# Attention feeding a gated product: four chunks of Strassen-like products run as one stream, with attention and checks dealt out as timed events

## The chip, the cores and the metric

One core of a Trainium2 chip. The metric is the device time of the whole program in microseconds, the median of the runs. TensorE (PE) does matrix products, VectorE (DVE) and ScalarE (ACT) read its results in PSUM, GpSimd (POOL) works in SBUF alone, and SyncE (SP) issues transfers. PSUM has eight banks, and each holds a tile of 128 x 512 fp32 values.

## The reference

Attention over 4 batches, 8 heads, 768 positions and head width 64, where a position sees the first `n_sink` (4) positions and a window of 128 before it; then a gated product on the result, without a nonlinearity:

```python
scores = np.where(is_sink | in_window, scale * (q @ k.T), -1e9)
a = softmax(scores)            # over the last axis, sum + 1e-9
x = (a @ v)                    # heads joined: 3072 tokens x 512
out = ((x @ w_a) * (x @ w_b)) @ w_out     # 512 -> 1536 -> 512
```

Inputs are fp32; the weights come as 64-bit words that the kernel turns into a high and a low fp16 part.

## The kernel before

Tokens are worked off in seven chunks (`CHUNKS`): 512 tokens, 256, 256, then four of 512. While the gated product of chunk c runs on TensorE, the attention for chunk c+1 is made in between, by a generator (`attention`, `pipeline`) that `run` advances in its function `between` after each group of matmuls. A *unit* of attention is one head and one tile of 128 queries: two score matmuls into the only PSUM bank with tag `s` (L600), on VectorE the mask and maximum (L608, L610), the exponential on ScalarE (L612), sum and reciprocal (L614, L615), the scaling (L620), two units later a transpose through TensorE (L644, L645 or L650, L651), and for each pair of heads the product with v (L515, L658) and the sinks' part (`sinks_t`, `sinks_av`: L665 to L679). GpSimd rounds and splits q and k (L450, L456).

Chunks 0 to 2 use the plain product (`moe`: L1031 the two input products, L1040 the output product), each fp32 product as three of fp16 parts. In chunk 0 the weights are loaded and converted besides, on VectorE and ScalarE (L399 to L419). Chunks 3 to 6 use seven products for a 2 x 2 block product (`moe_of_seven`: L924 the products, L934 the output projections). They need sums of weight blocks: `weight_sums` (L375 to L386) makes them in 84 units, one instruction each, 72 on VectorE and 12 on ScalarE; `ahead` calls for 42 in chunk 1 and 42 in chunk 2. They also need sums of the input's blocks, made by `split_sums` (L886 to L900) at the head of each chunk.

A chunk of seven has six steps p; each has the products 5, 1, 2, 6, 3, 7, 4 (12 matmuls of 256 columns each) into two banks, copies between the banks on ScalarE (L981, L985, L993), the two gates `even` and `odd` (L944 to L949), and their high and low fp16 parts (ScalarE L954, GpSimd L955). `out(i)` puts the four output projections (six matmuls of 512 columns each) of the step before between the products; the first step has none, and after the sixth the last four follow one another. `finish` then moves the four output banks out (L1080), stores them, and the sums of their squares follow in the next chunk (`sum_rows`, L1109).

Instructions stand in each engine's queue in an order that a scheduler works out from the program order and from modelled times: an instruction with nothing to wait for can be put ahead of its place. `keep_in_program_order` (`pin`) binds one behind the instruction written just before it on its engine. An engine works its queue off in order.

`check_weight` loads each weight once more in two halves (L437) and takes minimum and maximum on VectorE (L427, L429): 30 of the 36 in the last chunk, one each 9/5 slots of 66, looked at in the following slot; two in each of chunks 3, 4 and 5. The loads of heads (`kr`, `qr`, `vsr`) and of checks share six SBUF buffers (`io`).

Of the kernel before, what the change touches and what calls it, by code (L numbers as in the profile page):

```python
# [20 lines left out]
P = 128  # L21
# [215 lines left out]
SEVEN = 3  # L237
R = P * 2
RING = 4

class Fast:
# [120 lines left out]
    def weight_sums(self):  # L364

        nc = self.nc
        V = nc.vector
        for p in range(NJ // 2):
            self.sums[p] = self.wp.tile([P, 2, 4, 2, R], F16, tag=f"r{p}", name=f"sums{p}")
            for i, kind in enumerate("ab"):  # L370
                b = self.cp.tile([P, 4, R], F32, tag="blocks", name=f"blocks{kind}{p}")
                t = self.cp.tile([P, 4, R], F32, tag="turns", name=f"turns{kind}{p}")
                for d in range(2):
                    wh, wl = self.weight(kind, 2 * p + d)
                    V.tensor_tensor(b[:, 2 * d:2 * d + 2].rearrange("p a f -> p (a f)"), wh, wl, op=ALU.add)  # L375
                    yield
                V.tensor_tensor(t[:, 0:2], b[:, 2:4], b[:, 0::2], op=ALU.subtract)
# [3 lines left out]
                V.tensor_tensor(t[:, 3], b[:, 1], t[:, 2], op=ALU.subtract)  # L381
# [4 lines left out]
                V.tensor_tensor(s[:, :, 1], t, s[:, :, 0], op=ALU.subtract)  # L386
# [35 lines left out]
    def check_weight(self, kind, j):  # L422

        nc, pin = self.nc, self.tc.keep_in_program_order
        for raw, i in self.unchecked:
# [5 lines left out]
        self.unchecked = []  # L431
        if kind is None:
            return
# [85 lines left out]
    def attention(self, b, t0, nt, xf, heads=range(H), bank=None):  # L519
# [4 lines left out]
        return self.pipeline(units, nt, late, *parts, 2, 4, 1, self.tight)  # L524

    def attentions(self, segments, xf):

        gens, o = [], 0
        for b, t0, nt in segments:
            gens.append(self.attention(b, t0, nt, [x[:, o:o + nt * P] for x in xf]))  # L530
            o += nt * P
        for i, gen in enumerate(gens):
            n = self.steps(segments[i], self.tight) - (i > 0)
            for k in range(n):
                if k == n - 5 and i + 1 < len(gens):
                    next(gens[i + 1])
                next(gen)
                yield
            assert next(gen, "end") == "end"

    def steps(self, segment, apart):
        b, t0, nt = segment
        return H * nt + 7 + (10 if apart else 0)
# [282 lines left out]
    def pipeline(self, units, nt, late, do_prep, scores, transposes, av, sinks_t, sinks_av, lag, group, early, apart):  # L826
# [5 lines left out]
        for k in range(nu + lag + 2 + group // 2):  # L832
# [6 lines left out]
            if 0 <= n < nu and units[n][1] == nt - 1:  # L839
                h = units[n][0]  # L840
                av(h)
                if apart and h % 2:
                    yield
                if h % group == group - 1 and late:
                    sinks_t(h // group)
                    if apart:
                        yield
            for c in range(group // 2):
                n -= 1
                if 0 <= n < nu and units[n][1] == nt - 1:  # L850
                    h = units[n][0]
                    if h % group == group - 1 and late:
                        sinks_av(h // group, c)
                        if apart:
                            yield
# [21 lines left out]
    def split_sums(self, xf, tag):  # L877

        nc = self.nc
        V = nc.vector  # L880
        a11, a12, a21, a22 = (xf[:, 2 * k:2 * k + 2, e::2] for e in range(2) for k in range(2))
        xs = {}
# [11 lines left out]
        s2 = self.mo.tile([P, 2, R], F32, tag="g", name=f"s2_{tag}")  # L894
# [6 lines left out]
        split(7, a21)  # L901
        split(4, a22)
        return xs

    def moe_of_seven(self, segments, first, xf, between, ahead, last):
# [3 lines left out]
        tag = f"{first}"  # L909
        xs = self.split_sums(xf, tag)  # L910
        outs = [self.ps.tile([P, DM], F32, tag=("o0", "o1", "o2", "av")[i], name=f"o{tag}_{i}") for i in range(4)]
        places = []
# [46 lines left out]
        for p in range(NJ // 2):  # L959
# [7 lines left out]
            def out(i):  # L967
                if prev is not None:
                    project(i, *prev)
# [333 lines left out]
```

## Time and profile before

| | us |
|---|---|
| median of 3 runs | 753.59 (752.77 to 754.82) |
| the profiled execution | 755.17 |
| its span | 753.4 |
| TensorE busy | 701.5 |
| VectorE busy | 540.7 |
| ScalarE busy | 418.0 |
| GpSimd busy | 263.0 |

The profile is of one execution. The span runs from the program's first to its last instruction; the execution's own time has 1.8 us around it. Busy times are unions of an engine's instructions. TensorE's instructions overlap, so how fast it works is read from the time from one start to the next, or from runs of matmuls without a gap. Chunk c ends where the first product of the next begins: at 149.9, 231.2, 301.9, 418.6, 537.8 and 651.4 us for chunks 0 to 5, and the last matmul of chunk 6 ends at 746.4.

### The profile page before, as it was taken

Reading aid. Unit: us, or ns where it says so; the run is one execution under the profiler, and the core shown is the slowest. Engines: PE = TensorE matmul, PEld = TensorE weight load, DVE = VectorE, ACT = ScalarE, POOL = GpSimd, SP = SyncE. Lnnn points to the kernel's source line nnn. Section 1 sums busy time; section 2 is a strip of 40 time slices with the busy share of each in tenths; the row PEclk is TensorE's granted clock in tenths of the full one; section 3 lists DMA queues with packets and bytes.
Section 4 is the critical chain, followed back from the end, with each engine's and each line's share of the span. In section 5 each row is a group of like instructions: output and inputs, shape, how many; then the busy total and the mean of one; then the engine's idle time right before and its main releaser. Section 6 shows DMA issues by size and latency. Waiting matters only on the chain. (4 is left out here: it accounts for less than half of the span.)

```text
span 753.4 us, 14486 instructions
## 1 busy us (share of the span) xinstructions
PE 701.5 (93%) x4976; PEld 475.0 (63%) x4976; DVE 540.7 (72%) x1660; ACT 418.0 (55%) x1169; POOL 263.0 (35%) x312
## 2 busy tenths in 40 slices
PE   8999998979889999898999899999899999798996
PEld 5644444456656767676776576767577777576673
DVE  7999999999998565855555765664755653886653
ACT  6867877556447675755644654563666453422222
POOL 2200004127743664354441564673154511111111
PEclk9999999999999999999999999999999999999999
DMA  8566454012311222122110222142112010466521
GB/s 271 192 228 215 156 206 161 18 68 61 92 40 58 71 81 77 44 57 76 37 50 8 96 79 60 37 142 75 57 57 86 22 51 1 140 207 215 184 67 58
DMA packets 43533, 73.43 MB, mean 97 GB/s; under 512 B 4608, under 2 KB 21056, under 8 KB 43456
## 3 DMA queue, kind: packets, MB, share of 16 engines
q1 hardware_dynamic: 40208, 66.96, 28.2%
q10 hardware_dynamic: 3248, 5.51, 1.9%
q8 instruction: 40, 0.66, 0.4%
q14 instruction: 37, 0.30, 0.1%
HBM read 66.16 MB, written 6.29 MB: 96 GB/s over the span
## 5 line engine op out<-in xcount | busy, mean ns | idle before, releaser
L924 PEld LDWEIGHTS <-sums 128*128 128x128 f16 x1152 | 112.4, 99 | 24.2 <-issue 6.7
L934 PE MATMUL o<-wt,gh 128*128 128x512 f16 x384 | 115.2, 379 | 2.9 <-ACT gh L954 2.9
L955 POOL TENSOR_TENSOR gl<-g,gh 128x512 f16<-128x512 f32 x48 | 55.6, 1158 | 168.5 <-ACT gh L954 149.6
L1031 PEld LDWEIGHTS <-wt 128*128 128x128 f16 x864 | 82.9, 99 | 47.6 <-issue 5.7
L924 PEld LDWEIGHTS <-wt 128*128 128x128 f16 x864 | 83.1, 98 | 24.0 <-issue 7.2
L612 ACT ACTIVATE p<-p,st 128x136 f32<-128x136 f32 (+2 forms) x160 | 66.1, 413 | 45.8 <-DVE st L610 41.0
L1031 PE MATMUL b<-x,wt 128*128 128x256 f16 (+1 forms) x432 | 73.3, 312 | 3.5 <-DVE st L614 3.2
L924 PE MATMUL x<-x,sums 128*128 128x256 f16 x576 | 73.3, 275 | 3.6 <-DVE g L948 3.6
L924 PE MATMUL x<-x,wt 128*128 128x256 f16 x576 | 72.6, 273 | 2.6 <-ACT z L985 2.6
L934 PE MATMUL o<-wt,gl 128*128 128x512 f16 x192 | 72.8, 379 | 2.0 <-POOL gl L955 2.0
L1031 PE MATMUL a<-x,wt 128*128 128x256 f16 (+1 forms) x432 | 72.7, 309 | 1.9 <-ACT wt L414 1.4
L450 POOL TENSOR_SCALAR qh<-qr 128x256 fp32r<-128x256 f32 (+1 forms) x48 | 26.2, 545 | 135.9 <-PE s L600 94.1
L924 PE MATMUL z<-x,sums 128*128 128x256 f16 x576 | 73.4, 274 | 0.0
L600 PE MATMUL s<-ks,qh 128*128 128x264 f32 (+1 forms) x160 | 61.5, 384 | 9.4 <-DVE st L610 8.3
L620 ACT ACTIVATE p<-p,st 128x128 f32<-128x128 f32 x120 | 47.9, 399 | 35.5 <-DVE st L615 34.8
L954 ACT CAST gh<-g 128x512 f16<-128x512 f32 x48 | 29.6, 616 | 64.2 <-DVE g L949 55.5
L1040 PE MATMUL o<-wt,gh 128*128 128x512 f16 x192 | 60.3, 387 | 2.4 <-ACT wt L414 1.0
L456 POOL TENSOR_TENSOR ks<-kr,ks 64x400 fp32r<-64x400 f32 (+1 forms) x48 | 61.0, 1271 | 3.7
L608 DVE COPY_PREDICATED s<-mg,s 128x128 f32<-128x128 int32 x120 | 34.6, 288 | 32.7 <-PE s L600 32.7
L645 DVE TENSOR_TENSOR pt<-t,tri 128x256 f32<-128x256 f32 x120 | 50.1, 417 | 9.4 <-PE t L644 8.8
L934 PEld LDWEIGHTS <-gh 128*128 128x128 f16 x384 | 37.1, 99 | 31.0 <-ACT gh L954 4.3
L614 DVE TENSOR_SCALAR st<-st 128x1 f32<-128x1 f32 x160 | 23.9, 150 | 36.6 <-ACT p L612 36.0
(187 smaller groups left out, 1450.4 us busy)
## 6 DMA issues: line engine op xcount, KB each, us to landing
raw<-in_wa_dram SPq DMA_DIRECT2D x12, 512.0 KB, 4.6
raw<-in_wb_dram SPq DMA_DIRECT2D x12, 512.0 KB, 4.6
raw<-in_wo_dram SPq DMA_DIRECT2D x12, 512.0 KB, 4.3
qr<-in_qT_dram SPq DMA_DIRECT2D x24, 256.0 KB, 2.6
chk_b<-in_wb_dram SPq DMA_DIRECT2D x24, 256.0 KB, 3.2
chk_o<-in_wo_dram SPq DMA_DIRECT2D x24, 256.0 KB, 3.5
chk_a<-in_wa_dram SPq DMA_DIRECT2D x24, 256.0 KB, 3.3
out_dram<-os ACTq DMA_DIRECT2D x20, 256.0 KB, 2.1
```

What stands on the lines that cost most here:

```text
L456: self.nc.gpsimd.tensor_tensor(o, i, high.bitcast(F32), op=ALU.subtract)
L600: mm = nc.tensor.matmul(ps[:, :w], lhsT=q[:, i * P:(i + 1) * P], rhs=ks[:, c0:c0 + w], start=m == 0, stop=m == 1)
L608: nc.vector.copy_predicated(ps[:, KB:], self.up, ps[:, :P])
L612: nc.scalar.activation(p[:, :w], p[:, :w], AF.Exp, bias=st[:, 0:1], scale=-1.0, accum_out=st[:, 1:2])
L620: nc.scalar.mul(p[:, NS:KB], p[:, NS:KB], st[:, 3:4])
L645: nc.vector.tensor_tensor(pt[:, k:k + 2, :], tp[:, 0:1, :].broadcast_to([P, 2, P]), self.tri, op=ALU.mult)
L924: nc.tensor.matmul(ps[:, c * R:(c + 1) * R], lhsT=w[:, kk], rhs=y[:, kk], start=start and c == 0 and kk == 0 and i == 0, stop=c == 1 and k ...
L934: nc.tensor.matmul(outs[i], lhsT=g[:, d, sl], rhs=w, start=p == 0 and d == 0 and k == 0, stop=p == NJ // 2 - 1 and d == 1 and k == 2)
L954: nc.scalar.copy(gh, g[:, 0:2])
L955: nc.gpsimd.tensor_tensor(gl, g[:, 0:2], gh, op=ALU.subtract)
L1031: nc.tensor.matmul(ps[:, :n], lhsT=w[:, ksl], rhs=x[:, :n], start=kk == 0 and i == 0, stop=kk == NK - 1 and i == 2)
L1040: nc.tensor.matmul(outs[i], lhsT=g[:, sl], rhs=w, start=j == 0 and k == 0, stop=j == NJ - 1 and k == 2)
```

## The change

- The four chunks of seven become one loop, `sevens`. The four last projections of a chunk stand in the first step of the next, between its products; each output bank is moved out and stored at once (`evict`). Only the last chunk still has projections after its products.
- `split_sums` becomes a generator: the next chunk's sums are made in the last step of the chunk before, one after each product, in a buffer of their own.
- A step has 22 points (`point`), one in the middle and one at the end of each product and each projection, in place of 11 slots. Attention for the next chunk is a list of events with times in points (`events`): the first list takes the first 108 of 132 points, and each later one begins where the one before it ends, 24 points before the end of a chunk, and takes 132.
- `weight_sums` are bound in program order (`pin`): 28 units in chunk 1, 35 in chunk 2, 21 in the first three steps of chunk 3.
- Checks: one each 7/2 points in the last chunk, looked at six points later.
- In the last step of all, the low part of the last gate is made on VectorE, and the projections 2 and 3 use it last.

```diff
-SEVEN = 3
+SEVEN, STEPS, LAG = 3, 22, 2
+CHUNK = STEPS * NJ // 2
+EARLY, LOOK = 24, 6
...
-                V.tensor_tensor(t[:, 2], t[:, 1], b[:, 0], op=ALU.add)
+                pin(V.tensor_tensor(t[:, 2], t[:, 1], b[:, 0], op=ALU.add))
...
-        for raw, i in self.unchecked:
+        for raw, i in self.unchecked[:2] if kind is None else ():
-        self.unchecked = []
         if kind is None:
+            del self.unchecked[:2]
...
+    def events(self, segments, xf, begin, end):
+        lag = LAG
+        out, o = [], 0
+        scale = (end - begin) / (H * sum(n for _, _, n in segments) / 1 + lag + 5)
+        def add(t, f, *a):
+            out.append((begin + (t + 1.5) * scale, len(out), f, a))
+        for s, (b, t0, nt) in enumerate(segments):
+            prep, scores, transposes, av, sinks_t, sinks_av = self.parts_split(
+                b, t0, nt, Columns(xf, o * P, nt * P), range(H), None)
+            k0 = H * o
+            o += nt
+            late = self.late(b, t0, nt)
+            add(k0 - (2.4 if s else 1.5), prep, 0)
+            for h in range(H):
+                for i in range(nt):
+                    k = k0 + h * nt + i
+                    if i == 0:
+                        add(k, prep, h + 1)
+                    add(k, scores, h, i)
+                    add(k + lag + 0.01, transposes, h, i)
+                if h % 2:
+                    add(k + lag + 0.5, av, h)
+                if h % 4 == 3 and late:
+                    add(k + lag + 1.5, sinks_t, h // 4)
+                    for c in range(2):
+                        add(k + lag + 2.5 + c, sinks_av, h // 4, c)
+        return sorted(out, key=lambda x: x[:2])
...
-        s1 = self.mo.tile([P, 2, R], F32, tag="g", name=f"s1_{tag}")
+        s = self.cp.tile([P, 2, 2, R], F32, tag="blocks", name=f"s{tag}")
+        s1, s2 = s[:, 0], s[:, 1]
+        yield
+        yield
+        V.tensor_tensor(a21, a11, a21, op=ALU.subtract)
+        yield
-        V.tensor_tensor(a21, a11, a21, op=ALU.subtract)
+        yield
+        yield
...
+    def sevens(self, chunks, makes, point):
...
+        def step():
+            point(done[0])
+            done[0] += 1
...
+                if c == 0:
+                    step()
+                if d == 0 and prev:
+                    step()
+            if p == NJ // 2 - 1 and n + 1 < len(chunks):
+                self.evict(outs[n, i], *places(n)[i], f"{n}_{i}")
...
+        def out(i):
+            if prev:
+                project(i, *prev[0])
+            else:
+                step()
+            step()
...
+        for n in range(len(chunks)):
+            last = n + 1 == len(chunks)
+            for p in range(NJ // 2):
+                end = p == NJ // 2 - 1
+                splits = iter(()) if last or not end else self.split_sums(makes[n + 1], n + 1, ys)
...
+                products(z, p, 5, True)
+                next(splits, None)
+                fifth = self.mo.tile([P, 2 * R], F32, tag="fifth", name=f"fifth{name}", bufs=1)
+                nc.scalar.copy(fifth, z)
+                out(0)
+                x = self.ps.tile([P, 2 * R], F32, tag="a", name=f"x{name}")
+                products(x, p, 1, True)
+                next(splits, None)
+                nc.scalar.copy(z, x)
+                step()
+                out(1)
+                products(x, p, 2, False)
+                next(splits, None)
...
+                odd = parts(odd, f"o{name}", nc.vector if last and end else nc.gpsimd)
...
+                prev[:] = [(n, p, (even, odd))]
+            xs, ys = ys, {}
+        now = prev.pop()
+        for i in (0, 1):
+            project(i, *now)
+        for kinds in ((0, 1), (2,)):
+            for i in (2, 3):
+                project(i, *now, kinds)
+        self.finish([outs[n, i] for i in range(4)], places(n), f"{n}", True)
+    def evict(self, ps, place, k, name):
+        o = self.mo.tile([P, DM], F32, tag="os", name=f"os{name}", bufs=4)
+        self.nc.scalar.activation(o, ps, AF.Copy, scale=1.0 / (G_UP * W_UP))
+        self.nc.scalar.dma_start(place, o)
+        self.unsummed.append((o, k))
...
+        summed, shares = [0], (0, 28, 63, 84)
...
+                if c:
+                    sum_weights(shares[c - 1] + (shares[c] - shares[c - 1]) * (s + 1) // (3 * NJ))
...
+        for n, segments in enumerate(chunks[SEVEN + 1:], 1):
+            begin = (n - 1) * CHUNK - (EARLY if n > 1 else 0)
+            todo += self.events(segments, makes[n], begin, n * CHUNK - EARLY)
+        looks = []
+        def point(q):
+            sum_weights(shares[2] + (shares[3] - shares[2]) * (q + 1) // (3 * STEPS))
+            while todo and todo[0][0] <= q:
+                _, _, f, a = todo.pop(0)
+                f(*a)
+            if looks and looks[0] <= q:
+                looks.pop(0)
+                self.check_weight(None, 0)
+            if q in checks:
+                self.check_weight(*order[checks[q]])
+                looks.append(q + LOOK)
...
```

`Columns` is a lazily made view of the next chunk's input tile.

## Rows read from the trace of the kernel before

**Rows 1.** page, part 1: busy time of the engines, share of the span, instructions

```profile
PE 701.5 (93%) x4976; PEld 475.0 (63%) x4976; DVE 540.7 (72%) x1660; ACT 418.0 (55%) x1169; POOL 263.0 (35%) x312
```

**Rows 2.** stages: length; busy of PE, PEld, DVE, ACT, POOL; clock; DMA share; GB/s

```profile
33.50:149.90 116.40, 109.54 (x572) 53.13 (x570) 112.53 (x205) 82.24 (x173) 11.91 (x15) 1.00 0.47 159
149.90:231.20 81.30, 70.11 (x489) 48.05 (x488) 80.24 (x196) 42.84 (x118) 42.05 (x46) 0.96 0.21 64
231.20:301.90 70.70, 69.31 (x526) 50.22 (x525) 43.85 (x207) 47.45 (x166) 39.66 (x46) 1.00 0.25 72
301.90:418.60 116.70, 109.96 (x825) 79.84 (x824) 69.83 (x250) 65.27 (x194) 44.68 (x48) 1.00 0.16 48
651.40:746.40 95.00, 89.00 (x649) 63.96 (x647) 61.90 (x171) 25.00 (x49) 13.89 (x12) 0.98 0.49 158
```

**Rows 3.** groups of VectorE, chunk 1, then chunk 0: count, busy us, mean ns

```profile
L375 DVE TENSOR_TENSOR blocksa<-wt 128x512 f32<-128x512 f16 x10 | 9.9, 1004 | 0.0
L379 DVE TENSOR_TENSOR turnsb<-turnsb,blocksb 128x256 f32<-128x256 f32 x5 | 2.7, 532 | 0.0
...
L375 DVE TENSOR_TENSOR blocksb<-wt 128x512 f32<-128x512 f16 x2 | 1.4, 689 | 0.0
L386 DVE TENSOR_TENSOR sums<-turnsa,sums 128x1024 f16<-128x1024 f32 x1 | 1.2, 1217 | 0.0
L379 DVE TENSOR_TENSOR turnsa<-turnsa,blocksa 128x256 f32<-128x256 f32 x1 | 0.4, 406 | 0.0
```

**Rows 4.** timeline, chunk 1: start, length, engine, line

```profile
208.31 1.83 DVE L386 TENSOR_TENSOR sums<-turnsb,sums 128x1024 f16<-128x1024 f32 x1
209.14 2.17 POOL L456 TENSOR_TENSOR ks<-kr,ks 64x536 fp32r<-64x536 f32 x1
210.13 1.73 DVE L375 TENSOR_TENSOR blocksa<-wt 128x512 f32<-128x512 f16 x1
```

**Rows 5.** timeline, chunk 1: idle time and releaser at the end

```profile
164.36 2.52 PE L1031 MATMUL b<-x,wt 128*128 128x256 f16 x12 [3.20 <-DVE st L614]
```

**Rows 6.** timeline of TensorE, end of chunk 3 and start of chunk 4

```profile
415.24 0.60 PE L934 MATMUL o<-wt,gh 128*128 128x512 f16 x2 [0.95 <-ACT gh L954]
416.48 0.39 PE L934 MATMUL o<-wt,gl 128*128 128x512 f16 x1 [0.63 <-POOL gl L955]
...
422.71 0.49 PE L924 MATMUL x<-x,wt 128*128 128x256 f16 x3 [0.71 <-ACT z L985]
```

**Rows 7.** TensorE's waits, chunks 3 to 5: us, times, longest

```profile
PE s L600 <- DVE st L610: 4.1, 9, 0.8
PE t L644 <- DVE xf L679: 3.0, 2, 1.5
PE o L934 <- ACT gh L954: 2.9, 3, 1.0
PE o L934 <- POOL gl L955: 2.0, 3, 0.7
PE x L924 <- ACT z L985: 1.8, 3, 0.7
PE z L924 <- ACT x L993: 1.0, 2, 0.7
```

**Rows 8.** TensorE's waits, last chunk

```profile
PE x L924 <- DVE g L948: 3.6, 4, 2.0
PE z L924 <- ACT x L993: 1.6, 1, 1.6
```

**Rows 9.** chain that ended last, in order of time

```profile
652.23 5.32 DMA out_dram<-os
...
687.95 4.47 DMA chk_o<-in_wo_dram
...
720.25 1.30 PE o L934 x6
721.55 1.31 PE z L924 x12
```

More of the change, by code (lines that the diff above doesn't have):

```diff
@@ L523, in attention @@
         units = [(h, i) for h in heads for i in range(nt)]
[L524 to L543, printed above, removed]
+        return self.pipeline(units, nt, late, *parts, 2, 4, 1)
+    def events(self, segments, xf, begin, end):
[25 more added lines that the diff above has]
+        return sorted(out, key=lambda x: x[:2])
     def attention_in_one_bank(self, b, t0, nt, xf):
@@ L824, in first_attention, with pipeline @@
                 yield
-    def pipeline(self, units, nt, late, do_prep, scores, transposes, av, sinks_t, sinks_av, lag, group, early, apart):
+    def pipeline(self, units, nt, late, do_prep, scores, transposes, av, sinks_t, sinks_av, lag, group, early):
         for h, i in units[:early * nt:nt]:
@@ L1120, in run, with sum_weights @@
         done, loaded = [0], [0]
+        def sum_weights(n):
+            while summed[0] < min(n, shares[-1]):
+                next(sums)
+                summed[0] += 1
         def weights_to(n, ahead):
@@ L1145, in weights_to @@
                     self.weight_bits(k, 2)
-        last = len(chunks) - 1
-        checks = [(last, 9 * i // 5) for i in range(30)] + [(c, s) for c in range(SEVEN, last) for s in (22, 44)]
+        last = len(chunks) - 1 - SEVEN
+        checks = {(last * CHUNK) + 7 * i // 2: i for i in range(30)}
+        checks.update({c * CHUNK + 40 * d: 30 + 2 * c + d - 1 for c in range(last) for d in (1, 2)})
         (b, t0, nt), = chunks[0]
@@ L1166, in run @@
         sums = self.weight_sums()
-        summed, units = [0], 7 * NJ
+        summed, shares = [0], (0, 28, 63, 84)
         nxf = x
-        places = [16, 20, 22] + [4 * i for i in range(4)]
-        for c, segments in enumerate(chunks):
+        rows = (16, 20, 22)
+        for c in range(SEVEN):
+            segments = chunks[c]
             gen = None
@@ L1196, in between @@
                 if c:
[L1197 removed]
+                    want = min(steps, -(-steps * (s + 1) // (3 * NJ - 3)))
                 else:
@@ L1209, in ahead, with make @@
                     weights_to(max(s + AHEAD, done[0] + 1 - DELAY), LOADS)
-                if c in (1, 2):
-                    for _ in range(units * ((c - 1) * 3 * NJ + s + 1) // (6 * NJ) - summed[0]):
-                        next(sums, None)
-                        summed[0] += 1
-                if (c, s) in checks:
-                    self.check_weight(*order[checks.index((c, s))])
-                elif self.unchecked:
-                    self.check_weight(None, 0)
-            if seven:
-                self.moe_of_seven(segments, places[c], x, between, ahead, c + 1 == len(chunks))
-            else:
-                (b, t0, nt), = segments
-                self.moe(b * S + t0 * P, places[c], nt, xf, between, ahead, False, c > 0)
-            if gen is not None:
-                for _ in gen:
-                    pass
+                if c:
+                    sum_weights(shares[c - 1] + (shares[c] - shares[c - 1]) * (s + 1) // (3 * NJ))
+            (b, t0, nt), = segments
+            self.moe(b * S + t0 * P, rows[c], nt, xf, between, ahead, False, c > 0)
+            for _ in gen:
+                pass
+        self.tight = True
+        made = {0: nxf}
+        def make(n):
+            if n not in made:
+                made[n] = self.new_xf(SEVEN + n)
+            return made[n]
+        makes = [lambda n=n: make(n) for n in range(len(chunks) - SEVEN)]
+        todo = []
+        for n, segments in enumerate(chunks[SEVEN + 1:], 1):
[13 more added lines that the diff above has]
+                looks.append(q + LOOK)
+        self.sevens(chunks[SEVEN:], makes, point)
         return val, whole(self.good, self.ps.tile([1, P], F32, tag="s", name="gp"))
```

176 lines of the change are left out of this document (70 added, 106 removed).

## The prediction

> **What bounds the kernel now.** The page's busy line comes first [rows 1]: TensorE is busy 93% of the span, VectorE 72%. That average hides which engine sets each stage, so the busy table by stage comes next [rows 2]. With TensorE at full clock, 12 matmuls of 256 columns take 1.31 us and six of 512 columns 1.30 [rows 9]. A chunk of seven products has 42 products and 24 output projections: 42 x 1.31 + 24 x 1.30 = 86.2 us. The last chunk holds nothing else for TensorE and took 95.0 [rows 2]: 8.8 us to gain there. In chunk 2 TensorE is busy 69.3 of 70.7 us, so it is the bound. In chunk 1 it is busy 70.1 of 81.3 and its clock is granted at 0.96, while VectorE is busy 80.2 of 81.3: VectorE is the bound there, as it is in chunk 0 (112.5 of 116.4). The groups of VectorE instructions in chunk 1 say why [rows 3]: the weights' sums are ten groups, 60 instructions and 52.7 us, two thirds of all its work. The program deals them over chunks 1 and 2 alike, yet of 72 nine ran in chunk 0 (seven groups, 6.2 us) and only three in chunk 2: nothing held them in place. The other place is the seams between chunks: the timeline and TensorE's waits there [rows 6, 7].
>
> **The sums leave chunk 1.** 28 of the 84 units stay there; six in seven are VectorE instructions (the seventh is ScalarE's copy), so 24 instead of 60. Without the 36 VectorE's work falls from 80.2 by 36/60 x 52.7 = 31.6 to about 49 us, and TensorE sets the time again. Its idle time was 81.3 - 70.1 = 11.2. Clock 0.96 over 81.3 us is another 3.3: behind a wait of 3.20 us twelve matmuls took 2.52 us [rows 5], the lower level, 1.2 GHz, against 1.31 at 2.4 GHz; without such waits that goes as well. Of 14.5 I leave 2.2 as remaining waits, somewhat more than chunk 2 shows (1.4 idle): **-12.3 us** (bounds -8 to -14).
>
> Chunk 0: nine sums, 6.2 us, go from an engine busy 97%. Some stood where it would have idled, and the conversion of weights stays the bound: **-2.0** (0 to -6).
>
> **Where they go.** Chunk 2 gets 35 units, 30 VectorE instructions where three ran. A group of six costs undisturbed 3 x 0.69 + 2 x 0.42 + 1.22 = 4.1 us, 0.69 each; in chunk 1 it was 52.7/60 = 0.88 [rows 3]. VectorE's 43.9 us, less 2.1 for the three (1.2 + 2 x 0.4), rise by 20.7 to 26.4, to 62 to 68 us beside 69.3 of TensorE. It would be close to full, and the score tiles have one PSUM bank that only VectorE empties, so scores wait more often. From both sides: nothing if all fits; if VectorE sets the time as it did in chunk 1, 68 plus the few us that both engines lose to each other, about +9. I take **+4.8**.
>
> Chunk 3 gets the last 21 units, 18 instructions, 12.4 to 15.8 us, in its first three of six steps. VectorE's share of chunk 3 is 69.8/116.7, half of it 35 us per half chunk; attention is also denser (its events end at step 108 of 132, 82% of the chunk, where 62 of 66 slots, 94%, were used), 1.15 times; about half of the 35 is attention's, so +2.5. Some 50 to 53 of 57 us (a half of 116.7 is 58): **+4.4** (0 to +10).
>
> A rule bears on this. The row first: a sum beside a GpSimd instruction of 2.17 us took 1.83 and the next 1.73 [rows 4], where 1.22 and 0.69 are the undisturbed prices. The Trainium skill, "SBUF — State Buffer", section "SBUF: two separate sides", says that VectorE instructions with two SBUF inputs and GpSimd share a port pair that one locks for a whole instruction while the other fully blocks. The trace agrees with it. Sums and the gates' products are of this kind, and GpSimd is busier where the sums go (39.7 of 70.7 us) than where they were (42.1 of 81.3) [rows 2]. By this rule the excess of 0.19 per sum grows by 0.56/0.52, 30 sums cost some 27 us and chunk 2 sits at the upper bound; that is the rival "dear sums" below.
>
> **The seams.** Before, each chunk closes with four projections, two of which need the last gate. TensorE waits 0.95 us for ScalarE's high part and 0.63 for GpSimd's low part [rows 6]; 416.48 comes 1.24 after 415.24 where the two matmuls between take 0.43 (a third of 1.30), so the loss is 0.81, a little more than the idle time; with the like for the first wait it is 1.9 us a seam. Both waits come three times [rows 7]. With the next chunk's first products issued between, the gate has three products' time (4 us): 3 x 1.9 = 5.7 us go. A first step without projections also exposes ScalarE's copies between banks: 0.71 [rows 6], and over chunks 4 to 6 some 4.0 us of idle time (1.2 of the 1.8 and 0.5 of the 1.0 in rows 7 are those of chunks 4 and 5; chunk 6 has 1.6 [rows 8] and a wait of 0.7 like that of rows 6). The 1.6 comes from VectorE standing at the row sums of an output whose transfer took 5.32 us [rows 9]. With a projection between products these go too, but not in chunk 3, which has no predecessor in the stream. The old chunk's outputs now leave one by one, each summed a whole step later. What is late next: the next chunk's splits, eleven VectorE instructions of 512 columns (0.69 each as the sums' additions, 7.6 us) and seven ScalarE copies, move from the chunk's head into the last step (7 products and 4 projections, 14 us of TensorE), where they stand among the gates. Attention's last event comes some six half products before the first split; if it slips, gates wait behind splits. I give back 1.5 for the three seams (0 to 4). Sum **-8.2**.
>
> **The last chunk.** VectorE checks 30 weights there, two transfers each, looked at one slot after their issue. In the chain, transfers stand on the path for 4.47 us [rows 9] and once more like it, and TensorE waits 3.6 us for the gate queued behind these checks [rows 8]; the clock at 0.98 over 95 us is up to 1.9 more. Looking six half products later gives a transfer about 4 us, near what it took; four transfers are then in flight, in six buffers, so the SP queue need not stand for a buffer. **-4.2** of 5.5 (0 to -5.5).
>
> **Edits taken near nothing.** The tail: banks 2 and 3 get their low parts at the very end, so bank 2 closes four 512-column matmuls (0.87 us) later and its eviction with it; the low part on VectorE, idle there, takes GpSimd off: **+0.4** (0 to +0.9). Attention as events: the same matmuls, exits and transfers in the same order with the sinks a unit apart, where the waits [rows 7] show 4.1 us for scores and 3.0 for the shared bank in three chunks: 0 (-4 to +3), since a finer grain shortens waits for VectorE and the shared bank stays. The DMA issues of heads and checks remain on SP in the same number; their cover is attention's lead of one head.
>
> **Sum.** -12.3 - 2.0 + 4.8 + 4.4 - 8.2 - 4.2 + 0.4 = -17.1. The profiled execution took 755.2 us (span 753.4), the median of the runs is 753.6, so 738.1 by the one and 736.5 by the other: I say **736.5**. My own range, from the middling bounds, is 729 to 744.
>
> **Rivals.**
> - *Free sums.* VectorE has room in chunks 2 and 3 (62 of 69 us), the 9.2 us given back fall to 1 or 2, and chunk 0 gains 1 more: 753.6 - 26.3 + 1.5 - 1 = 728. For it: chunk 2's waits are few now. Against: one bank for scores. 20%.
> - *Dear sums.* Lengthened by GpSimd's work, the sums fill VectorE, and chunks 2 and 3 cost their upper bounds, 9 and 10 in place of 4.8 and 4.4: 753.6 - 26.3 + 19 = 746. For it: the long sums [rows 4]; against: at 62 to 68 of 74 us VectorE is not yet full. 17%.
> - *Sums not spread.* A binding to the instruction ahead does not help if that one also floats forward; then only seams and last chunk gain, 12: 741.6; within my range. For it: the nine in chunk 0 floated; against: an instruction ahead stands near its own place. 5%.
> - *Slower.* Each sum stands in TensorE's way for its own length: 48 of them newly placed between a score and its exit x 0.88 = 42 us, against 26.3 gained elsewhere: 753.6 + 16 = 770. It decides from 26.3/48 = 0.55 us lost per sum on. Against it: chunk 1 lost 14.5 us to 60 of them, 0.24 each, with VectorE full. 8%.
> - The forecast: 46%; 4% for other ways to about no change (attention late at each seam, seams 5 us worse, with dear sums).
>
> **How the numbers follow.** The range takes in free and dear sums with their bounds: 723 to 749. From no change a measurement here can tell 0.3%, 2.3 us. Faster has forecast, free and dear sums and the unspread case, 88%; the same 3%; slower 9%.
>
> **What would show it.** Chunk 1 about 69 us at clock 1.00 with VectorE under 75% there; sums between 150 and 360 us, 30 in chunk 2; chunk 2 at 74 to 77 us; no wait of a projection for a high or low part at a seam; each inner chunk of the stream 112 to 116 us; no check's transfer on the chain. It is wrong if chunk 2 or the first half of chunk 3 lengthens by 10 us or more, if splits hold TensorE at each seam, or if VectorE still stands for transfers in the last chunk.

## The result and the profile after

The kernel after takes 741.62 us (740.96 to 744.8) against 753.53 us (752.77 to 754.82) on the same chip: a ratio of 0.9849, 95% interval 0.9817 to 0.988. Its profiled execution took 741.34 us, with a span of 739.6. That is 13.8 us less span than before, while the medians differ by 11.9, because the profiled execution of before stood 1.6 us above its median. The forecast was 736.5. In the sum's own currency, profiled execution against profiled execution, it was 738.1 and the run 741.3: 3.2 us were not gained.

Lengths of the stages in us, from the first product of a chunk to that of the next, in the profiled executions (the start-up differs from run to run, 33.4 to 36.9 in all the profiles, with nothing changed in it; where the program and the granted clock are the same, stages agree within 0.1, as chunks 0 to 3 of "more buffers" below do with those of after):

| | start | 0 | 1 | 2 | 3 | 4 | 5 | 6 | tail | span |
|---|---|---|---|---|---|---|---|---|---|---|
| before | 33.5 | 116.4 | 81.3 | 70.7 | 116.8 | 119.1 | 113.6 | 94.9 | 7.1 | 753.4 |
| after | 33.7 | 120.5 | 61.2 | 78.0 | 118.8 | 116.4 | 106.7 | 97.2 | 7.3 | 739.6 |

Three shifts of work have to be read out of it first. Chunk 0 is 4.1 us longer and busier on TensorE, because 24 more of its matmuls now stand ahead of chunk 1's first product; chunks 0 and 1 count together, 197.7 and 181.7. And the four last projections of each chunk (5.2 us) now stand in the next one: chunk 3 has 5.2 us less to do and chunk 6 5.2 us more, 86.2 + 5.2 = 91.4 at full rate. So chunk 6 lost 94.9 - 86.2 = 8.7 us before and loses 97.2 - 91.4 = 5.8 now. Third, each later list of events begins 24 points before the end of a chunk: chunk 3 now holds 76 score matmuls, 18.8 us of TensorE's busy time, where it had 64 and 16.2, and chunk 5 holds 52 and 13.1, where it had 64 and 16.0.

The page's busy line of after, in the form of [rows 1]:

```profile
PE 697.1 (94%) x4976; PEld 474.5 (64%) x4976; DVE 551.6 (75%) x1661; ACT 416.7 (56%) x1169; POOL 265.9 (36%) x311
```

The stages of after that answer to [rows 2] (stretch, length, busy us of PE, PEld, DVE, ACT, POOL, clock, DMA share, GB/s):

```profile
33.70:154.10 120.40, 114.12 (x596) 55.47 (x594) 112.03 (x202) 84.35 (x177) 11.40 (x14) 1.00 0.46 155
154.10:215.30 61.20, 59.77 (x465) 44.26 (x464) 48.69 (x150) 32.95 (x107) 36.04 (x47) 1.00 0.28 83
215.30:293.30 78.00, 72.65 (x526) 50.11 (x525) 66.15 (x237) 50.34 (x169) 46.45 (x46) 1.00 0.23 66
293.30:412.10 118.80, 109.28 (x816) 79.22 (x817) 90.66 (x294) 70.05 (x211) 50.40 (x56) 1.00 0.16 47
635.20:732.40 97.20, 92.41 (x674) 65.61 (x671) 63.63 (x179) 27.39 (x52) 14.10 (x13) 1.00 0.50 163
```

Chunk 1 went as foretold: VectorE fell from 80.2 to 48.7 us, TensorE is busy 59.8 of 61.2, and the clock rose from 0.96 to 1.00 (with the 5.2 us that moved to chunk 0 it is 66.4 us, where the prediction had about 69). Chunks 2 and 3 have VectorE at 66 of 78 and 91 of 119 us, and that is where part of the gain goes back.

The seam between chunks 3 and 4, TensorE's timeline in after (start, length, engine, line, tiles; in brackets the idle time before it and its releaser):

```profile
411.55 0.36 PE L622 MATMUL s<-ks,qh 128*128 128x264 f32 x1 [1.37 <-DVE st L632]
...
412.10 0.82 PE L947 MATMUL z<-x,sums 128*128 128x256 f16 x6
...
414.54 0.59 PE L962 MATMUL o<-wt,ghe 128*128 128x512 f16 x2
414.97 0.38 PE L962 MATMUL o<-wt,gle 128*128 128x512 f16 x1
```

The old chunk's projection (414.54) follows the new chunk's product without waiting for a high or a low part; both waits of [rows 6] are gone. What is left there is a score tile that waits for VectorE.

The last chunk is the other place. TensorE's waits of after there (us in all, times, longest), against 3.6 for the gate in [rows 8]:

```profile
PE x L947 <- DVE go L986: 4.7, 5, 1.7
```

And the chain that ended last, in order of time, which answers to [rows 9] (start, length, what):

```profile
638.64 4.00 DMA out_dram<-os
...
642.77 0.69 DVE os L1156
...
659.22 2.96 DMA chk_a<-in_wa_dram
...
675.88 4.23 DMA chk_b<-in_wb_dram
...
680.47 0.69 DVE go L986
...
692.11 3.46 DMA chk_b<-in_wb_dram
```

The chain still passes through an output's transfer (4.00 us) into its row sum, and now through three of the checks' transfers, where it had two. VectorE stands for transfers in that chunk for 9.9 us in all (4.3 for the output, 5.6 for checks), where it stood 5.2 before: of what the prediction named as a sign of being wrong, this one came.

### The profile page after: what moved, and what is told of

It is laid out like the page before. It is cut to its first block, busy times and chain, and to the rows that moved or that the text cites. A ratio compares the mean times of both kernels' runs of the same rounds, so it can differ in the third digit from the quotient of the medians.

```text
span 739.6 us, 14457 instructions
## 1 busy us (share of the span) xinstructions
PE 697.1 (94%) x4976; PEld 474.5 (64%) x4976; DVE 551.6 (75%) x1661; ACT 416.7 (56%) x1169; POOL 265.9 (36%) x311
## 4 chain that ended last, share of the span: by engine, by line
PE 51%; DVE 33%; ACT 7%; DMA 4%; issue 4%; SPq 1%; ACTq 0%; DVEq 0%
PE x L947 12%; PE o L962 11%; PE z L947 8%; PE av L525 4%; PE s L622 4%; PE a L1078 3%; PE o L1087 3%; PE b L1078 2%; DVE wf L418 2%; DVE p L632 2%; DVE wf L411 2%; DVE go L987 2%; PE t L666 1%; DVE x L903 1%; DVE wt L429 1%
## 5 line engine op out<-in xcount | busy, mean ns | idle before, releaser
L947 PEld LDWEIGHTS <-sums 128*128 128x128 f16 x1152 | 112.0, 99 | 27.9 <-issue 10.6
L634 ACT ACTIVATE p<-p,st 128x136 f32<-128x136 f32 (+2 forms) x160 | 66.2, 413 | 43.9 <-DVE st L632 42.7
L947 PE MATMUL z<-x,sums 128*128 128x256 f16 x576 | 77.1, 275 | 1.1 <-DVE st L636 0.9
L993 POOL TENSOR_TENSOR gle<-ge,ghe 128x512 f16<-128x512 f32 x24 | 28.4, 1182 | 116.1 <-ACT ghe L992 99.4
L1087 PE MATMUL o<-wt,gh 128*128 128x512 f16 x192 | 58.5, 380 | 0.2 <-DVE wt L429 0.2
L962 PE MATMUL o<-wt,ghe 128*128 128x512 f16 x192 | 57.7, 380 | 0.0
L962 PE MATMUL o<-wt,gho 128*128 128x512 f16 x192 | 56.8, 379 | 0.0
L466 POOL TENSOR_TENSOR ql<-qr,qh 128x256 fp32r<-128x256 f32 (+1 forms) x48 | 51.6, 1075 | 2.1
L993 POOL TENSOR_TENSOR glo<-go,gho 128x512 f16<-128x512 f32 x23 | 27.5, 1194 | 67.1 <-ACT gho L992 57.9
L622 PEld LDWEIGHTS s<-ks,qh 128*128 128x128 f32 x160 | 30.2, 189 | 31.3 <-DVE st L632 13.3
```

Of the source, the lines that this page charges most:

```text
L466: self.nc.gpsimd.tensor_tensor(o, i, high.bitcast(F32), op=ALU.subtract)
L622: mm = nc.tensor.matmul(ps[:, :w], lhsT=q[:, i * P:(i + 1) * P], rhs=ks[:, c0:c0 + w], start=m == 0, stop=m == 1)
L634: nc.scalar.activation(p[:, :w], p[:, :w], AF.Exp, bias=st[:, 0:1], scale=-1.0, accum_out=st[:, 1:2])
L947: nc.tensor.matmul(ps[:, c * R:(c + 1) * R], lhsT=w[:, kk], rhs=y[:, kk], start=start and c == 0 and kk == 0 and i == 0, stop=c == 1 and k ...
L962: nc.tensor.matmul(outs[n, i], lhsT=g[:, d, sl], rhs=w, start=p == 0 and d == 0 and k == 0, stop=p == NJ // 2 - 1 and d == 1 and k == 2)
L993: engine.tensor_tensor(gl, g[:, 0:2], gh, op=ALU.subtract)
```

## The experiments

All ratios are to the kernel before on the same chip, with 95% intervals. Edits are against the kernel after unless it says otherwise. In the expectations the chunks of seven products are at places counted within the four (0 to 3), which are chunks 3 to 6 here.

### The sums: is it the binding, and what do they still cost?

**One part alone**: the kernel before with its sums bound in order (42 units in chunk 1, 42 in chunk 2), nothing else.

```diff
-                V.tensor_tensor(t[:, 0:2], b[:, 2:4], b[:, 0::2], op=ALU.subtract)
+                pin(V.tensor_tensor(t[:, 0:2], b[:, 2:4], b[:, 0::2], op=ALU.subtract))
...
```

> The kernel before with one edit: the weights' sums bound in program order, 42 units dealt to chunk 1 and 42 to chunk 2; no stream, no events. Theory (VectorE was full in chunks 0 and 1, nothing held the sums back, and sums in a stage that VectorE does not fill cost about 0.24 us of TensorE's time each): chunks 0 and 1 together fall from 197.7 us by 11 to 15, since 36 VectorE sums stay in chunk 1, chunk 2 grows from 70.7 by 7 to 9, chunk 3 is unchanged; together 4 to 7 us faster than before, 746 to 750. Rival (the sums cost the same wherever they stand, the gain came from the stream): no change within 2 us, 752 to 756.

Measured: 755.08 us, ratio 1.0002 (0.998 to 1.0024). No change. Its stages, 120.5, 67.2, 79.5, 119.5, say why: chunks 0 and 1 gain 10.0, chunk 2 gives back 8.8 and chunk 3 2.7, of which some 1.8 is the clock (0.90 in its first step of 17.9 us). In that kernel the sums are moved, not hidden. Its chunk 6, which the edit does not touch, took 92.5 us at clock 1.00, where the kernel before had 94.9 at 0.98; that is needed below.

**One part undone**: the kernel after with its sums not bound.

```diff
-                pin(V.tensor_tensor(t[:, 0:2], b[:, 2:4], b[:, 0::2], op=ALU.subtract))
+                V.tensor_tensor(t[:, 0:2], b[:, 2:4], b[:, 0::2], op=ALU.subtract)
...
```

> The changed kernel with one edit undone: the weights' sums not bound, dealt 28, 35 and 21 as changed. Theory: the scheduler puts them forward again into chunks 0 and 1, VectorE is full there (80 of 81 us), chunks 0 and 1 take 194 to 198 us instead of 181.6, chunk 2 falls to about 71 and chunk 3's first half by about 5: together 2 to 6 us slower than the changed kernel, 743 to 748. Rival (binding is worth its full 16 us in chunks 0 and 1 and costs nothing later): 757. Rival (binding does nothing): 741.6.

Measured: 745.43 us, 0.9868 (0.9845 to 0.9892), an interval that overlaps that of after. The binding does hold the sums in place: of VectorE's 72, chunks 0 to 3 ran 9, 45, none and 18 here, and none, 24, 29 and 19 in after. By stages (116.4, 76.6, 73.1, 117.4, then as after) it is worth 11.3 us in chunks 0 and 1 and costs 4.9 and 1.4 in chunks 2 and 3: 5.0 us in all, by one execution, in which the clock was 0.98 in chunk 1 and 0.99 in chunk 3.

**The cost taken away**: the arithmetic of the sums.

```diff
-                    pin(V.tensor_tensor(b[:, 2 * d:2 * d + 2].rearrange("p a f -> p (a f)"), wh, wl, op=ALU.add))
...
+                nc.gpsimd.memset(self.sums[p][:, i].bitcast(F32), 0.0)
...
```

> The changed kernel without the arithmetic of the weights' sums: each sums tile is set to zero by GpSimd, 12 instructions in place of 84 (this part of the computation is left out, all else and all matmuls stay). It shows what the sums still cost. Theory (each VectorE sum costs TensorE about 0.27 us in chunk 2 and in the first half of chunk 3, as 30 sums cost 7.3 us in chunk 2, and nothing in chunk 1 any more): chunk 2 back to 70.5 to 72, chunk 3 to 112 to 114, chunk 1 within 1.5 of 61.2; 11 to 14 us faster than the changed kernel, 727 to 731. Rival (chunk 3 is longer because attention there is denser, not by its sums): chunk 3 stays above 117, 6 to 8 us faster.

Measured: 725.02 us, 0.9619 (0.9587 to 0.965). Stages 121.1, 58.3, 73.1, 110.3: 2.9 us less in chunk 1, 4.9 in chunk 2 and 8.5 in chunk 3, more than I expected in chunks 1 and 3. Chunks 2 and 3 of this kernel, in the columns of the stage rows above:

```profile
214.50:287.70 73.20, 70.94 (x532) 50.78 (x531) 44.82 (x209) 48.44 (x169) 39.48 (x46) 1.00 0.23 70
287.70:398.00 110.30, 105.73 (x812) 79.22 (x811) 73.55 (x271) 65.27 (x203) 49.33 (x56) 1.00 0.17 51
```

The line between the two chunks does not lie at the same place in the work. Here chunk 2's last six projection matmuls run before chunk 3's first product, in after they run behind it (timelines, first of this kernel, then of after):

```profile
286.32 0.60 PE L1073 MATMUL o<-wt,gh 128*128 128x512 f16 x2 [0.87 <-ACT gh L1092]
...
287.66 1.47 PE L933 MATMUL z<-x,sums 128*128 128x256 f16 x12
```

```profile
293.28 0.28 PE L947 MATMUL z<-x,sums 128*128 128x256 f16 x1
...
294.09 0.81 PE L1087 MATMUL o<-wt,gh 128*128 128x512 f16 x3
```

Six matmuls are 1.3 us. Counted alike, the sums still cost 6.2 us in chunk 2 (0.21 for each of the 29 that ran there) and 7.2 in chunk 3 (0.38 for each of 19).

TensorE's waits in chunk 2, of after and of this kernel:

```profile
PE s L622 <- DVE st L632: 3.2, 6, 1.0
```

```profile
PE o L1073 <- ACT gh L1092: 0.9, 1, 0.9
```

With sums TensorE's longest wait is for the one score bank, six times; without them no such wait is left. Without the sums chunk 2's VectorE is at 44.8 us, beside them at 66.2.

**Spread further**: the last 21 units over 100 points in place of 66.

```diff
-            sum_weights(shares[2] + (shares[3] - shares[2]) * (q + 1) // (3 * STEPS))
+            sum_weights(shares[2] + (shares[3] - shares[2]) * (q + 1) // 100)
```

> The changed kernel with the last 21 steps' worth of weights' sums of the seven-product chunks (the part that is dealt out in chunk 3) spread over 100 half products in place of 66. Theory: VectorE was nearly full in the first half of chunk 3 (52.4 of 61.7 us busy) and less so in the second (38.2 of 57.1), and the sums' price there (8.5 us for 18 of them) is that of the crowding; spread, chunk 3 takes 115 to 117 us in place of 118.8, the time is 738 to 740 us. Rival: each sum costs TensorE a fixed 0.47 us wherever it stands in the chunk, and chunk 3 stays at 118.8 +- 0.5 us: 741.5 us.

Measured: 743.11 us, 0.9853 (0.9821 to 0.9885); chunk 3 took 120.0 us. The last sum ran 90.8 us into the chunk in place of 62.5, and nothing came back: the theory of a crowded first half fell. Why a sum costs nearly twice as much here as in chunk 2 stays open.

### The seams

**Undone**: a chunk's four last projections again right behind its products.

```diff
+            if not last:
+                now = prev.pop()
+                for i in range(4):
+                    project(i, *now)
```

> The changed kernel with the last four projections of each chunk again behind its products; splits, events, checks and sums as changed. Theory (seam stalls are 1.9 us for the last gate's parts and 0.7 to 1.7 for the bank copies of a first step without projections): three seams times 2.6 to 3.6 us, 8 to 11 us slower than the changed kernel, 749 to 753. Rival (the gate's wait at the seam was covered by other losses, or comes back elsewhere): under 3 us slower.

Measured: 751.41 us, 0.9937 (0.9908 to 0.9965). Chunks 3 to 6 take 8.9 us more (124.5, 118.0, 112.0, 93.4). TensorE's waits in chunks 4 and 5 bring both kinds back, for the last gate's parts and for the copies between banks:

```profile
PE x L947 <- ACT z L1015: 1.9, 3, 1.2
...
PE o L962 <- POOL glo L993: 1.6, 3, 0.7
...
PE o L962 <- ACT gho L992: 0.4, 2, 0.2
```

Not all of the 8.9 us is the seams'. In the first two steps of chunk 3 both kernels run the same instructions in the same order, with the same wait of 1.53 us for a copy in the first, and yet this run took 3.2 us more there, at a lower granted clock (this run, then after, in the columns of the stage rows):

```profile
294.60:337.40 42.80, 37.49 (x258) 27.01 (x259) 34.15 (x109) 25.11 (x77) 15.78 (x15) 0.92 0.14 45
```

```profile
293.30:332.90 39.60, 34.23 (x257) 25.07 (x258) 34.12 (x109) 25.01 (x77) 15.78 (x15) 1.00 0.15 48
```

The kernel after lost 1.6 us to its clock in turn, in the two steps around the seam of chunks 4 and 5; "spread further" runs the same instructions there in the same order (after, then that run):

```profile
507.80:547.70 39.90, 36.74 (x268) 27.29 (x266) 28.04 (x91) 25.01 (x71) 14.61 (x15) 0.96 0.17 54
```

```profile
512.60:550.90 38.30, 35.12 (x268) 26.39 (x267) 27.67 (x91) 24.95 (x71) 14.66 (x15) 1.00 0.18 56
```

With the clock full on both sides the seams are worth 8.9 - 3.2 + 1.6 = 7.3 us. The ratios to the kernel before, 0.9937 here and 0.9849 and 0.9866 for after, say 5.4 to 6.6, each with an interval of some 3 us.

**The next chunk's splits** at that chunk's head again, the rest as after:

```diff
+            for _ in self.split_sums(makes[n], n, xs) if n else ():
+                pass
...
-                splits = iter(()) if last or not end else self.split_sums(makes[n + 1], n + 1, ys)
+                splits = iter(())
```

> The changed kernel with the sums of the input's blocks made at the head of each chunk again, the last projections still in the first step. Theory (the seam's gain comes from the projections, which gives the copies and gates cover; the splits are covered at either place as long as x5, the first, is ready, about 2 us of VectorE and ScalarE after the head): TensorE waits 1 to 2.5 us for the first split at each of three seams, 3 to 7 us slower than the changed kernel, 745 to 749. Rival (splits at the head are hidden by the attention's and projections' matmuls that the scheduler has in the queue): within 1.5 us. Rival (they crowd the last step's gates more than they gain): 1 to 3 us faster.

Measured: 741.96 us, 0.9827 (0.9788 to 0.9866); the kernel after took 743.08 (0.9866, 0.9831 to 0.9901) beside it. The profile has 0.9 us more in chunk 3, which is less than the 1.6 that its clock cost in the second step (0.93), and 1.3 in chunk 6. No difference that can be told.

### The checks of the last chunk

In the kernel after, VectorE, SP and TensorE between 675 and 683 us (timeline):

```profile
675.88 0.98 SPq L447 DMA_DIRECT2D chk_b<-in_wb_dram  x2
676.10 0.41 DVE L439 TENSOR_REDUCE chk<-chk_b 128x1 f32<-128x256 f32 x1
...
677.71 0.42 DVE L987 SCALAR_TENSOR_TENSOR ge<-ge 128x256 f32<-128x256 f32 x1
...
680.13 0.42 DVE L437 TENSOR_REDUCE chk<-chk_b 128x1 f32<-128x256 f32 x1 [2.00 <-DMA chk_b<-in_wb_dram]
680.47 0.68 DVE L986 TENSOR_TENSOR go<-x,fifth 128x512 f32<-128x512 f32 x1
...
681.20 1.47 PE L947 MATMUL x<-x,sums 128*128 128x256 f16 x12 [1.72 <-DVE go L986]
```

SP issues a load at 675.88, when a burst of reductions has just given a buffer back; the load takes 4.23 us; the reduction that needs it stands in VectorE's queue ahead of gate `go`; VectorE idles 2.00 us for it and TensorE 1.72 for the gate. SP's own waits for a reduction, 69.5 us in 47 times, look longer than the 39.7 in 40 of before, but one of them, of 31.0 us, began at 606.8, before the chunk; without it they are 38.5 in 46. SP stands as long as it did.

**More buffers**: four more for the checks in the last chunk (the tiles of q, free by then), ten in all.

```diff
-            raw = self.io([P, DM], I32, f"chk_{kind}{j}_{d}")
+            if self.more and self.turn % 5 > 2:
+                raw = self.sp.tile([P, DM], I32, tag=("qh", "ql")[d], name=name)
+            else:
+                raw = self.io([P, DM], I32, name)
...
```

> The changed kernel with four more buffers for the checks' loads in the last chunk (the idle attention buffers qh and ql in two of five checks), ten in place of six. Theory (the loads wait for a buffer that is freed by a reduction standing behind a gate in VectorE's queue, so they land late and the next gate waits behind them): TensorE's 4.7 us of waits for the gate in the last chunk fall under 1.5, 3 to 5 us faster than the changed kernel, 736.5 to 738.5. Rival (the transfers themselves are too slow, or the reductions fill VectorE): no change within 1 us, 741 to 742.

Measured: 747.82 us, 0.9891 (0.9863 to 0.9919), chunk 6 103.1 us in place of 97.2: the opposite of what I expected. Its timelines, of SP and of VectorE:

```profile
669.48 1.97 SPq L451 DMA_DIRECT2D chk_a<-in_wa_dram  x2
671.50 0.90 SPq L451 DMA_DIRECT2D chk_b<-in_wb_dram  x2
...
674.35 1.28 SPq L451 DMA_DIRECT2D chk_b<-in_wb_dram  x2
```

```profile
680.93 0.42 DVE L437 TENSOR_REDUCE chk<-chk_b 128x1 f32<-128x256 f32 x1 [6.62 <-DMA chk_b<-in_wb_dram]
```

Ten loads go out within six microseconds. The first lands 2.6 us after its issue and the last two some 6.5; VectorE stands 6.62 us for one of these. More room made a larger burst here.

**Fewer loads there**: 18 weights checked in the last chunk in place of 30, one each six points, and eight in each of chunks 4 and 5 in place of two.

```diff
-        checks = {(last * CHUNK) + 7 * i // 2: i for i in range(30)}
-        checks.update({c * CHUNK + 40 * d: 30 + 2 * c + d - 1 for c in range(last) for d in (1, 2)})
+        when = [40, 80] + [c * CHUNK + 16 * d for c in (1, 2) for d in range(8)] + [last * CHUNK + 6 * i for i in range(18)]
+        checks = {q: i for i, q in enumerate(when)}
```

> The changed kernel with 18 of the 36 checks in the last chunk, one each 6 points, 8 each in chunks 4 and 5, two in chunk 3 as before. Theory (in the last chunk the loads come in bursts of up to six, since VectorE frees their buffers in bursts behind a gate, and 15.7 MB in about 68 us leave no room to catch up; ten buffers made longer bursts and longer landings): waits for the gate in the last chunk fall from 4.7 us under 1.5 and chunk 6 from 97.2 to 92.5 to 94, chunks 4 and 5 lengthen by under 2 together; 2 to 4 us faster than the changed kernel, 738 to 740. Rival (24 more reductions a chunk cost in chunks 4 and 5 what they free in the last): no change within 1 us.

Measured: 736.93 us, 0.9773 (0.9738 to 0.9808), beside 743.08 for the kernel after. Chunk 6 falls by 2.2 us to 95.0, less than I expected, with TensorE's waits for the gate at 1.7 us in place of 4.7, and chunks 4 and 5, which got twelve more weights, are not longer (115.2, 105.1). The median load of each weight kind lands 2.7 to 2.9 us after its issue, where it was 3.3 to 4.0. The rest of the gain lies in chunks 1 and 3 to 5; part of it is the clock, 1.00 at the seam of chunks 4 and 5 where after had 0.96.

### Attention as events

**Coarser**: events dealt out at every second point, two points' worth at a time.

```diff
-            while todo and todo[0][0] <= q:
+            while todo and todo[0][0] <= q and q % 2:
```

> The changed kernel with the attention's events dealt out at every second point only, two points' worth at a time, in all inner chunks. Theory: chunks 4 and 5, which became some 9.6 us shorter from the kernel before (119.1 + 113.6) to the one after (116.4 + 106.7), owe about 5 us of that to the finer grain of the events; dealt at every second point they take 2 to 5 us more, and the time is 743.5 to 746.5 us. Rival: the grain is worth nothing (what the prediction took), the 5 us came with the move of the last output products, and the stages stay within 0.5 us each: 741 to 742.5 us.

Measured: 741.28 us, 0.9822 (0.9791 to 0.9852). Chunk 3 is 1.5 us shorter, chunks 4 and 5 1.6 longer, so the stages moved by more than the rival allowed, but in sum the grain is worth nothing.

### Towards a better version

**Spread checks and late sums** together: 

> The two together: the checks' reads spread over the run (2 in chunk 0, 8 in each of chunks 1 and 2, 18 in the last chunk in place of 30), and the sums of chunk 3 spread over 100 half products. If both gains stand beside each other, 732 to 734.5 us, with chunk 3 at 115 to 117 us; if the late sums are worth nothing, that of the spread checks alone, 736 to 737 us.

Measured: 738.81 us, 0.9806 (0.9774 to 0.9837); chunk 3 119.2: slower than either expectation. The late sums add nothing to the spread checks.

**Shares and row sums moved**: that, and fewer sums in chunk 3, and an output's row sum one step later, bound there.

```diff
-        summed, shares = [0], (0, 28, 63, 84)
+        summed, shares = [0], (0, 32, 70, 84)
...
-                if self.unsummed:
+                if p and self.unsummed:
...
-                    self.sum_rows(o, o, k)
+                    self.tc.keep_in_program_order(self.sum_rows(o, o, k))
```

> The one before, with the sums dealt 32, 38 and 14 to chunks 1, 2 and 3 in place of 28, 35 and 21, and the row sums of an output issued one step later and bound in program order. Theory by the measured prices of a step's sums (0.10 us in chunk 1, 0.14 in chunk 2, 0.40 in chunk 3 for each of the units dealt out): chunk 3 gains 2.8 us, chunks 1 and 2 lose 0.8 us, so 2 us less than the kernel with spread checks and late sums. Rival: chunk 1 is already at its limit (59.8 of 61.2 us busy on TensorE, VectorE at 48.7), the four units more tip it over, and chunks 1 and 2 give back 2 to 4 us: the same or slower.

Measured: 731.51 us (727.83 to 731.58), 0.9682 (0.965 to 0.9715): the best of all. Chunks 1, 2, 3 and 6 take 60.6, 75.7, 116.4 and 91.8 us. Chunk 3's 2.8 less is near what a price of 7.2/21 = 0.34 a unit gives for seven units (2.4), but the row sums of chunk 2's outputs were moved there too, and the two edits are not told apart. Chunk 6's 2.7 less are the row sums', since no weights' sums stand there, and with them VectorE's wait of some 4 us ahead of a row sum is gone. That chunks 1 and 2 are shorter with more sums in them, chunk 2 by 2.3 us with 31 in place of 29, I did not expect. No row sum was moved there, so it is the dealing of the sums: a sum has no fixed price, and what sets it is not shown. Its last chunk, as a stage and by TensorE's waits:

```profile
630.90:722.70 91.80, 91.61 (x674) 65.64 (x671) 52.26 (x131) 27.22 (x52) 14.12 (x13) 1.00 0.32 104
```

```profile
PE x L947 <- DVE go L986: 0.2, 1, 0.2
```

TensorE is busy 91.61 of 91.80 us, 0.4 from the 91.4 that its work takes at full rate, and VectorE waits for no transfer there any more. The 8.7 us to gain in that chunk were real (2.4 of them the clock's, as the binding alone shows), and it took two edits that this change did not have.

## Why the prediction was right in sign and 3 us off in its terms

The direction and the main mechanism held: the sums left chunk 1, the seams closed, and the time lies between the forecast and "dear sums". "Sums not spread" names the same 741.6 us and is refuted all the same: 29 sums ran in chunk 2, of 30 dealt to it. Between the medians the forecast is 5.1 us off; 1.9 of these come from an execution of before that stood above its median. Term by term, in profiled time, with the kernel whose seams are undone as the step between before and after:

| term | forecast | measured | from |
|---|---|---|---|
| chunks 0 and 1 | -14.3 | -16.1 | stages |
| chunk 2 | +4.8 | +7.3 | stages; of it the sums 6.2 |
| chunk 3 | +4.4 | +4.6 | seams undone against before, 7.8 less 3.2 of clock; the sums 7.2 |
| seams | -8.2 | -7.3 | seams undone against after, at full clock |
| clock at a seam | 0 | +1.6 | after, seam of chunks 4 and 5 |
| last chunk's checks | -4.2 | -1.5 | the same step, chunk 6: 94.9 to 93.4 |
| events | 0 | -2.7 | the same step, chunks 4 and 5: 232.7 to 230.0 |
| tail | +0.4 | +0.3 | stages, start-up and tail |
| sum | -17.1 | -13.8 | |

With seams undone, twelve projection matmuls (2.6 us) of chunk 3 run behind chunk 4's first product, and as many of chunk 4 in chunk 5; the moved score matmuls (2.6 to 2.9 us busy) go the other way, from chunk 5 into chunk 3. In the rows for chunk 3 and for events the two nearly cancel.

- *Chunk 3 came out near its forecast, but not by its reasoning.* The step "12.4 to 15.8 us, in its first three of six steps" went on to a half chunk of 50 to 53 us of VectorE out of 57 and gave +4.4. VectorE was as full as I had it (52.4 of 61.7 us in the first half), the sums alone cost 7.2, and the rest of the chunk became some 2.6 shorter, which the forecast did not have: the hit is luck. Spreading the sums over more of the chunk gave nothing back, so that they are cheap because VectorE is not yet full was the wrong reasoning.
- *Chunk 2's price was mis-sized.* The sums cost TensorE 6.2 us in place of 4.8, and VectorE 28.5 us for 29 (0.98 each), beyond the 26.4 that the forecast had as its upper bound for 30. The other 1.1 us stay when the sums are taken out (71.8, the six projection matmuls counted alike, against 70.7); no run tells what they belong to.
- *The checks failed as a step.* "Four transfers are then in flight, in six buffers, so the SP queue need not stand for a buffer": it stood as long as before, because a load can go only when the reductions of an earlier one have run, and these stand in bursts behind a gate. TensorE's waits for the gate did not fall either: 3.6 us before, 4.2 with seams undone, 4.7 in after, with three transfers on the chain in place of two. The 1.5 us that chunk 6 gained in that step are its clock. The binding alone has the old checks and the same matmuls there, at the same clock as the run with seams undone, and is 0.9 us shorter (the binding alone, then seams undone; before in [rows 2]):

```profile
656.30:748.80 92.50, 87.30 (x649) 63.15 (x647) 61.73 (x171) 24.83 (x47) 13.90 (x12) 1.00 0.51 163
```

```profile
649.10:742.50 93.40, 87.61 (x649) 63.22 (x647) 60.27 (x170) 24.24 (x46) 12.71 (x11) 1.00 0.49 159
```

- *"With a projection between products these go too"* held for TensorE's waits for copies in chunks 5 and 6 (one of 1.2 us is left in chunk 4), and not for VectorE: it still stands 4.33 us at the row sum of an output on its way out (the 4.00 us transfer on the chain). Binding that sum a step later took 2.7 us from chunk 6.
- *Splits* cost 0 to 2 us in place of 1.5, by a comparison that can't tell them from nothing. *Events* were put at 0 (-4 to +3), since "the shared bank stays", and chunks 4 and 5 gained 2.7. Their grain is not the cause. The two waits for the shared bank in [rows 7], 1.5 us in each of chunks 3 and 5, are gone in after and with seams undone, and coarser events have one of 0.6; that may be part of it, and no run tests it alone.

Of the rivals "dear sums" came nearest: the sums themselves cost 13.4 us in chunks 2 and 3, where the forecast had 9.2 and this rival 19. That binding alone, in the kernel before, came out at no change points the same way: work taken from a stage where VectorE is the bound is not free where TensorE is.

## What to carry to other kernels

Price work that is moved by what it costs where it arrives, and measure that by taking it out: here a VectorE instruction of about 1 us cost TensorE 0.21 us in one stage and 0.38 in another, with VectorE full in neither, and less where it was dealt otherwise. Loads that wait for their predecessors' readers gained nothing here from a later look or from more buffers, which gathered the issues into a larger burst; fewer loads in the chunk did help, and so did a reader that no longer stood ahead of critical work in an in-order queue. Undo each part on its own before calling a sum right: three terms here missed by 2.5 to 2.7 us, one of them to the other side, and the total by 3.3. And before the length of a stage is put down to an edit, look at its clock and at which matmuls ran in it: 3.2 us of the seams' 8.9, and all that the checks seemed to gain, were clock.

## What the runs showed of the hardware

A sum of 0.41 us undisturbed took 1.91 beside two GpSimd instructions, VectorE's and GpSimd's timelines of after:

```profile
272.80 1.91 DVE L389 TENSOR_TENSOR turnsb<-turnsb,blocksb 128x256 f32<-128x256 f32 x1
```

```profile
272.56 0.63 POOL L460 TENSOR_SCALAR ks<-kr 64x536 fp32r<-64x536 f32 x1
273.16 1.26 POOL L466 TENSOR_TENSOR ql<-qr,qh 128x512 fp32r<-128x512 f32 x1
```

It ends (274.71) only after the second of them (274.42). This is the lock that the Trainium skill describes ("SBUF — State Buffer", "SBUF: two separate sides"), and the trace agrees, as far as GpSimd's times, which a profile gives roughly, can show it. Over chunk 2 the 29 sums took 0.98 us each where the undisturbed price is 0.69, and the run without sums adds the other side, GpSimd's 46 instructions of that chunk at 39.5 us in place of 46.5.

The same 256 KB load took a median of 2.7 to 2.9 us from issue to landing where the last chunk moved some 100 GB/s (fewer loads), 3.3 to 4.0 at 163 GB/s (the kernel after) and up to 6.6 when ten were issued within six microseconds (more buffers).

The granted clock of one and the same stretch of instructions can differ from run to run: chunk 3's first two steps ran at 1.00 in after and at 0.92 with seams undone, with the same wait of 1.53 us in them, and took 39.6 and 42.8 us.
